# First loads in order of need on two queues, the fourth token tile transposed by DMA, and the last q tiles in passes of 128

## The chip, the cores and the metric

The kernel runs on one core of a Trainium2 chip. The time is device microseconds for one execution.

In the profile PE is TensorE's matmuls, PEld its weight loads, DVE is VectorE, ACT is ScalarE, SP is SyncE. "SPq" and "ACTq" are the sequencers of SyncE and ScalarE when they issue DMA. Times are microseconds from the start of the span.

## The reference

Two layers, each of a dilated sliding attention block and a gated feed-forward block, on 2048 tokens of width 1024. Both blocks add to the residual `x`, and both start with a layernorm.

```python
def _A_ref(x, wqkv, wo):            # attention: 32 heads of 32, window of 8 keys, step 2
    qkv = (x @ wqkv) ...            # q, k, v
    ...                             # softmax over the 8 keys, weighted sum of v
    return o @ wo
def _B_ref(x, w1, w3, w2):
    return (silu(x @ w1) * (x @ w3)) @ w2
x = x + _A_ref(_layernorm(x), wqkv, wo)
x = x + _B_ref(_layernorm(x), w1, w3, w2)
x = x + _A_ref(_layernorm(x), wqkv, wo)
x = x + _B_ref(_layernorm(x), w1, w3, w2)
```

## The kernel before

Tokens go in chunks of 512, that is four tiles of 128 (0 to 3). Everything is recorded as operations with an assumed length and with the keys they read and write. A list scheduler, `place()`, simulates the engines with these lengths and writes the instructions in the order that its simulation gives. The order on each engine is fixed by the simulation, not by what is ready on the chip. And an `after=` key that a load does not really read gives no wait on the chip: it only moves the load later in the issue order.

```python
def place(self, n_banks=8, rate=330e3):
    engines = ("PE", "DVE", "ACT", "SP", "AQ", "POOL")   # AQ: DMA issued by ScalarE
    ...                                                   # earliest start first; PE has lanes
    placed.sort(key=lambda o: (o.start, o.seq))

def dma(kb, dst, src, reads, writes, cls=3, transpose=False, queue="SP"):
    def emit(op):
        if queue == "AQ":
            nc.scalar.dma_start(dst, src)
        elif transpose:
            nc.sync.dma_start_transpose(dst, src)
        else:
            nc.sync.dma_start(dst, src)
    return pr.add(queue, 0.45, emit, reads, writes, cls, size=kb * 1024)
```

The start of the kernel is written by hand. The q weights come as eight "rows" of 256 KB (row k holds 128 input channels). Tiles 0 and 1 are projected with only the mean taken off (their scale is put in later), one row at a time, so that TensorE can start before all weights are there. Tiles 2 and 3 are normalised first. Then K and V of the chunk follow with full-width matmuls of 512 columns; K's weights are two loads of 1 MiB, which I call K's first and second half.

```python
def q_first():
    for hh in range(2):                                   # x0 in halves, on the two queues
        dma(128, x_sb[0][:, ...], xin[:, 0, ...], [], [("x", 0, hh)], 0, queue="AQ" if hh else "SP")
    dma(256, x_sb[1][:], xin[:, 1, :], [], [...], 0, queue="AQ")
    rows = q_weights(0, "k", load=False)
    for kk in range(4):
        rows[2](kk)                                       # rows 0 to 3, SyncE
    load_x(0, 2, 4)                                       # x2, x3, SyncE
    rows[2](4)
    rows[2](5)
    ...
    rows[2](6, 2, queue="AQ", after=[("part", 1)])        # rows 6 and 7, ScalarE
    ...
    for j in range(2, TPC):                               # tiles 2 and 3
        stats(j); root(j, j + 1); apply(j)
        transposed(xn[j], ...)                            # on TensorE, copied by DVE and ACT
    for j in range(2):                                    # tiles 0 and 1, for K and V
        ...
        dma(256, xnT[b][:, :, j * P:(j + 1) * P], xn[j][:], [("xn", j)], [("xnT", b, j)], 0, transpose=True)
    ...
    for g in range(4):                                    # q of tiles 2 and 3: 64 matmuls of 256 columns
        ...
    wslots[1] = q_weights(1, "s")                         # K's weights, two halves of 1 MiB
```

Of the kernel before, what the change touches and what calls it, by code (L numbers as in the profile page):

```python
# [156 lines left out]
def kernel(  # L157
# [11 lines left out]
    nc = tc.nc  # L169
    P = 128  # L170
    _, S, D = A_x.shape
    F = B_w1.shape[1]
    KT = D // P
# [41 lines left out]
    wo = alloc("wo", [P, KT, D])  # L215
# [38 lines left out]
# [9 lines that stand above are left out]
# [34 lines left out]
    def load_x(c, j0=0, j1=TPC, after=()):  # L297
        for j in range(j0, j1):
            n = c * TPC + j
            dma(256, x_sb[n][:], xin[:, n, :], after, [("x", n, 0), ("x", n, 1)], 0 if c == 0 else 3)  # L300
# [3 lines left out]
    def ln(c, first=False):  # L304
        s = stage_no[0]
        b, q = s % 2, s % 4
        xb = xnT[b]

        def stats(j, after=()):
            n = c * TPC + j  # L310
            pri = -9 if first else 1
            for hh in range(2):
                dve(0.67, lambda _, hh=hh: nc.vector.bn_stats(st[q][:, j, hh, :],  # L313
                                                              x_sb[n][:, hh * 512:(hh + 1) * 512]),
                    [("x", n, hh)] + list(after), [("st", q, j, hh)], pri)
            dve(0.2, lambda _: nc.vector.bn_aggr(mv[q][:, j, :], st[q][:, j, :, :]),  # L316
                [("st", q, j, 0), ("st", q, j, 1)], [("mv", q, j)], pri)

        def root(j0, j1):
            act(0.3, lambda _: nc.scalar.activation(sd[q][:, j0:j1], mv[q][:, j0:j1, 1], ACTF.Sqrt, bias=epst[:]),  # L320
                [("mv", q, j) for j in range(j0, j1)] + ["eps"], [("sd", q, j) for j in range(j0, j1)], -9 if first else 0, table="sqrt")
            dve(0.16, lambda _: nc.vector.reciprocal(rstd[q][:, j0:j1], sd[q][:, j0:j1]),
                [("sd", q, j) for j in range(j0, j1)], [("rstd", q, j) for j in range(j0, j1)], -9 if first else 0)

        def apply(j):
            n = c * TPC + j
            dve(0.5, lambda _: nc.vector.tensor_scalar(xn[j][:], x_sb[n][:], mv[q][:, j, 0:1], rstd[q][:, j:j + 1],  # L327
                                                       op0=ALU.subtract, op1=ALU.mult),
                [("x", n, 0), ("x", n, 1), ("mv", q, j), ("rstd", q, j)], [("xn", j)] + [("xn", j, h) for h in range(2)], -9 if first else 1)

        if first:
            return b, q, stats, root, apply
        for j in range(TPC):
            stats(j)
        root(0, TPC)
        for j in range(TPC):
            apply(j)
            dma(256, xb[:, :, j * P:(j + 1) * P], xn[j][:], [("xn", j)],
                [("xnT", b, j)] + [("xnT", b, j, h) for h in range(2)], 0, transpose=True)
        return b  # L340
# [14 lines left out]

    wslots = {}

    def q_weights(which, split, load=True, after=()):
        ids = [take_slot(), take_slot()]
        if not load:  # L360
            def row(kk, n=1, after=(), **kw):
                i = ids[kk // 4]
                v = slot[i][:].rearrange("p (k c) -> p k c", k=4)
                dma(256 * n, v[:, kk % 4:kk % 4 + n, :], wqkv_v[:, kk:kk + n, which * D:(which + 1) * D], after,
                    [("w", i, kk % 4 + z) for z in range(n)], 0, **kw)
            return ids, split, row
        for h, i in enumerate(ids):
            if split != "c":
                v = slot[i][:].rearrange("p (k c) -> p k c", k=4)
                dma(1024, v, wqkv_v[:, 4 * h:4 * h + 4, which * D:(which + 1) * D], after,  # L370
                    [("w", i, k) for k in range(4)], 3)
            else:
                v = slot[i][:].rearrange("p (k c) -> p k c", k=KT)
                dma(1024, v, wqkv_v[:, :, which * D + h * 512:which * D + (h + 1) * 512], [],
                    [("w", i, k) for k in range(4)], 3)
        return ids, split

    def q_lhs(ws, kk, m):
        ids, split = ws
        if split == "s":  # L380
            i = ids[kk // 4]
            return slot[i][:].rearrange("p (k c) -> p k c", k=4)[:, kk % 4, m::KT], ("w", i, kk % 4)
        if split == "k":
            i = ids[kk // 4]
            return slot[i][:].rearrange("p (k c) -> p k c", k=4)[:, kk % 4, m * P:(m + 1) * P], ("w", i, kk % 4)
        i = ids[m // 4]
        return (slot[i][:].rearrange("p (k c) -> p k c", k=KT)[:, kk, (m % 4) * P:(m % 4 + 1) * P],
                ("w", i, kk // 2))
# [47 lines left out]
    def q_first():  # L436
# [3 lines left out]
        dma(256, x_sb[1][:], xin[:, 1, :], [], [("x", 1, 0), ("x", 1, 1)], 0, queue="AQ")  # L440
        rows = q_weights(0, "k", load=False)
        wslots[0] = rows[:2]
        for kk in range(4):
            rows[2](kk)
        load_x(0, 2, 4)
        rows[2](4)
        rows[2](5)
        b, q, stats, root, apply = ln(0, first=True)
        ce = hT[:, 8:16, :]
        dve(0.45, lambda _: nc.vector.tensor_scalar(xn[2][:, 0:512], x_sb[0][:, 0:512], 0.0, 0.0, op0=ALU.add,  # L450
# [1 line left out]
            [("x", 0, 0)], [("xn", 2), ("part", 0)], -9)  # L452
        act(0.75, lambda _: nc.scalar.activation(xn[3][:, 0:512], x_sb[0][:, 512:1024], ACTF.Copy,
                                                 accum_out=part[:, 1:2]), [("x", 0, 1)], [("xn", 3), ("part", 1)], -9)
        rows[2](6, 2, queue="AQ", after=[("part", 1)])
        dve(0.16, lambda _: nc.vector.tensor_scalar(mean[:, 0:1], part[:, 0:1], part[:, 1:2], 1.0 / D, op0=ALU.add,
                                                    op1=ALU.mult), [("part", 0), ("part", 1)], [("mean", 0)], -9)
        act(1.15, lambda _: nc.scalar.activation(xn[3][:], x_sb[1][:], ACTF.Copy, scale=1.0 / D,
# [7 lines left out]
            transposed(xn[j], [("xn", j, h) for h in range(2)], ce[:, :, j * P:(j + 1) * P],  # L466
                       [("ce", j, k) for k in range(KT)])
        for j in range(2, TPC):
            stats(j)
            root(j, j + 1)  # L470
            apply(j)
            transposed(xn[j], [("xn", j)] * 2, xnT[b][:, :, j * P:(j + 1) * P],
                       [("xnT", b, j, k // 4) for k in range(KT)])
        for j in range(2):
            act(1.25, lambda _, j=j: nc.scalar.activation(sgt[j][:].rearrange("p a b -> p (a b)"), x_sb[j][:],
                                                          ACTF.Square, bias=mean[:, j:j + 1], scale=-1.0,
# [37 lines left out]
        store(pa, [op] * 4, 0)  # L514
        pa = [Acc() for _ in range(4)]
        ops = []
        for g in range(4):
            lk = [[q_lhs(wslots[0], kk, m)[0] for kk in range(KT)] for m in (2 * g, 2 * g + 1)]

            def emit(op, g=g, lk=lk, pa=pa):  # L520
                for m in range(2):
                    for kk in range(KT):
                        nc.tensor.matmul(bank[pa[g].bank][:, m * 2 * P:(m + 1) * 2 * P], lhsT=lk[m][kk],  # L523
                                         rhs=xnT[b][:, kk, 2 * P:4 * P], start=(kk == 0 and m == 0),
                                         stop=(kk == KT - 1), skip_group_check=True)
            ops.append(pr.add("PE", 16 * 0.1092, emit,
                              [("w", i, k) for i in wslots[0][0] for k in range(4)] +
                              [("xnT", b, j, h) for j in (2, 3) for h in range(2)],
                              [], takes=[pa[g]], lag=0.17))
        store(pa, ops, 2)  # L530
        for m0 in range(0, KT, 2):
            dma(256, spill_view(0, 0, m0, 0), hT[:, m0:m0 + 2, :],
                [("hT", m, j) for m in (m0, m0 + 1) for j in range(TPC)], [("d", 0, 0, 0, m0)], 1)
        wslots[1] = q_weights(1, "s")
        load_x(1, 0, 4, [("xn", 1)])
        load_x(2, 0, 2, [("xn", 1)])
        wslots[2] = q_weights(2, "s", after=[("xn", 1)])
        load_x(2, 2, 4, [("hT", 7, TPC - 1)])
        load_x(3, 0, 4, [("hT", 7, TPC - 1)])
        for which, key, tile_ in ((1, "kT", kT), (2, "vT", vT)):  # L540
            dve(0.11, lambda _, tile_=tile_: nc.vector.memset(tile_[:, :, 0:HALO], 0.0), [], [(key, "h")], 1)
            q_tile(0, 0, which, wslots[which], b, (key, tile_))
        for t0, t1_ in ((0, 2), (2, 4), (4, 5), (5, 6), (6, 7), (7, 8)):
            dma(256 * (t1_ - t0), wo[:, t0:t1_, :], wo_v[:, t0:t1_, :], [("d", 0, 2, 0, 6)], [("wo", t0)], 3)
        stage_no[0] += 1

# [24 lines left out]
    def t_stage(l, half):  # L571
# [54 lines left out]
        for j in range(TCH // P):  # L626
            n = tok0 // P + j
            for hh in range(2):
                a = Acc()
                op = mm8(a, [(oT[oh][:, t, j * P:(j + 1) * P], wo[:, t, hh * 512:(hh + 1) * 512]) for t in range(KT)],  # L630
                         True, True, [("oT", oh, t) for t in range(KT)] + [("wo", t) for t in (0, 2, 4, 5, 6, 7)], lane=1)
                xs = x_sb[n][:, hh * 512:(hh + 1) * 512]
                evac(dve, t1(512), lambda _, xs=xs, a=a: nc.vector.tensor_tensor(xs, xs, bank[a.bank][:], op=ALU.add),  # L633
                     op, [("x", n, hh)], [("x", n, hh)], a)
# [126 lines left out]
```

## Time and profile before

| | before |
|---|---|
| median, 6 runs | 1616.09 us (1615.79 to 1616.38) |
| span of the profiled run | 1614.2 us |
| PE busy | 1601.5 us (99%) |
| first full-width matmul (K of chunk 0) | 22.54 us |
| last matmul starts | 1611.16 us |

The page's first part gives each engine's busy time, its share and its instructions. Its fourth part is the chain of work that ended last. Of the kernel before:

```profile
PE 1601.5 (99%) x7463; PEld 762.6 (47%) x7610; DVE 1121.5 (69%) x1904; ACT 331.3 (21%) x527; POOL 5.2 (0%) x28
...
PE bank L347 98%; DMA slot<-in_A_wqkv_dram 1%; PE bank L523 0%; PE bank L509 0%; PE bank L428 0%; SPq L261 0%; DVE x L688 0%
```

L347 is the helper that makes all full-width matmuls. The one other item with a share is the DMA that brings the q weights. The timeline of the same kernel (start, duration, engine, line, operation, count, and in brackets the idle time of the engine before it with what ended it) shows where:

```profile
5.89 1.05 PE L509 MATMUL bank<-hT,slot 128*128 128x128 bf16 x16 [0.25 <-DVE hT L433]
6.96 0.62 PE L428 MATMUL bank<-ident,xn 128*128 128x128 bf16 x8
7.42 2.83 PE L509 MATMUL bank<-hT,slot 128*128 128x128 bf16 x40
11.16 2.79 PE L509 MATMUL bank<-hT,slot 128*128 128x256 bf16 x24 [0.91 <-DMA slot<-in_A_wqkv_dram]
13.79 1.06 PE L428 MATMUL bank<-ident,xn 128*128 128x128 bf16 x16
14.68 1.04 PE L509 MATMUL bank<-hT,slot 128*128 128x256 bf16 x8
15.56 7.15 PE L523 MATMUL bank<-xnT,slot 128*128 128x256 bf16 x64
22.54 22.82 PE L347 MATMUL bank<-xnT,slot 128*128 128x512 bf16 x102
```

L509 is the q of tiles 0 and 1, L428 are transposes, L523 is the q of tiles 2 and 3. There is one wait of size, 0.91 us for q weights. From 22.54 us on TensorE does not pause: the sum of its matmuls at their own pace is 1588.6 us, and the last one starts 1588.6 us later.

SyncE's issues in the same timeline:

```profile
5.71 1.97 SPq L261 DMA_DIRECT2D slot<-in_A_wqkv_dram  x4
13.87 3.85 SPq L259 DMA_TRANSPOSE xnT<-xn  x2
17.77 2.94 SPq L261 DMA_DIRECT2D x<-in_A_x_dram  x6
```

The four loads issued from 5.71 us are rows 4 and 5 and both halves of K's weights, the last that K needs from HBM. Then SyncE stands until tile 0 is normalised, and issues two DMA transposes.

### The profile page before, as it was taken

The page shows a single profiled execution, that of the slowest core. Times are in us where ns is not written, and L with a number is a line of the kernel's source. Part 1 is how long each engine was busy: PE and PEld are TensorE (multiplying, and loading weights), DVE is VectorE, ACT ScalarE, POOL GpSimd, SP SyncE. Part 2 cuts the span into 40 slices and gives each one's busy share as a digit, 9 for nine tenths or more (in the row PEclk, how much of TensorE's full clock was granted, in tenths as well). Part 3 has the DMA queues.
Part 4 walks back from the last instruction along what each step waited for, and adds up shares of the span by engine and source line. Part 5 has one row for each costly group of instructions (what it writes and reads, how often), then busy time and mean ns, then how long its engine had stood idle before and what let it go on. Part 6 is the DMA issues. An engine that isn't in the chain of part 4 may idle for free.

```text
span 1614.2 us, 19079 instructions
## 1 busy us (share of the span) xinstructions
PE 1601.5 (99%) x7463; PEld 762.6 (47%) x7610; DVE 1121.5 (69%) x1904; ACT 331.3 (21%) x527; POOL 5.2 (0%) x28
## 2 busy tenths in 40 slices
PE   9999999999999999999999999999999999999999
PEld 6555544444444444444444444444444444444444
DVE  5898888889889888888898729884288832211211
ACT  5423322021211222113211032110321101101110
POOL 1000000000000000000000000000000000000000
PEclk9999999999999999999999999999999999999999
DMA  9834755395548664758645487365873464454451
GB/s 320 228 100 150 224 170 171 118 225 168 171 136 251 195 190 132 217 167 234 189 136 160 160 243 231 122 173 176 253 221 119 158 181 156 144 176 150 156 165 44
DMA packets 350777, 285.80 MB, mean 177 GB/s; under 512 B 72288, under 2 KB 344928, under 8 KB 350688
## 3 DMA queue, kind: packets, MB, share of 16 engines
q1 hardware_dynamic: 350128, 283.67, 58.2%
q8 instruction: 59, 0.97, 0.2%
q10 hardware_dynamic: 560, 0.92, 0.2%
q14 instruction: 30, 0.25, 0.0%
HBM read 238.94 MB, written 29.36 MB: 166 GB/s over the span
## 4 chain that ended last, share of the span: by engine, by line
PE 99%; DMA 1%; issue 0%; SPq 0%; DVE 0%
PE bank L347 98%; DMA slot<-in_A_wqkv_dram 1%; PE bank L523 0%; PE bank L509 0%; PE bank L428 0%; SPq L261 0%; DVE x L688 0%
## 5 line engine op out<-in xcount | busy, mean ns | idle before, releaser
L347 PE MATMUL bank<-xnT,slot 128*128 128x512 bf16 x4955 | 1088.9, 379 | 5.3
L347 PEld LDWEIGHTS <-slot 128*128 128x128 bf16 x5056 | 518.1, 102 | 573.0
L347 PE MATMUL bank<-slot,hT 128*128 128x512 bf16 (+2 forms) x1812 | 387.3, 372 | 1.9
L658 DVE TENSOR_TENSOR hT<-sg,bank 128x512 bf16<-128x512 bf16 x224 | 153.4, 685 | 213.0 <-PE bank L347 196.3
L265 DVE TENSOR_TENSOR scr<-scr 128x1024 bf16<-128x1024 bf16 (+3 forms) x576 | 292.1, 535 | 2.1
L347 PEld LDWEIGHTS <-hT 128*128 128x128 bf16 x1848 | 178.5, 98 | 208.7
L656 ACT ACTIVATE sg<-bank 128x512 bf16<-128x512 f32 x224 | 133.8, 597 | 653.8 <-PE bank L347 613.6
L265 DVE TENSOR_TENSOR scr<-qT,kT 128x2048 bf16<-128x2048 bf16 x128 | 153.7, 1216 | 71.7 <-DMA kT<-qkv_d 70.1
L405 ACT CAST sgt<-bank 128x512 bf16<-128x512 f32 x184 | 107.9, 586 | 290.9 <-PE bank L347 273.1
L265 DVE TENSOR_TENSOR scr<-pA,vT 128x2048 bf16<-128x2048 bf16 x128 | 152.5, 1216 | 0.4
L688 DVE TENSOR_TENSOR x<-x,bank 128x512 bf16<-128x512 bf16 (+1 forms) x66 | 43.7, 669 | 122.7 <-PE bank L347 122.4
L347 PE MATMUL bank<-wo,oT 128*128 128x512 bf16 x502 | 112.6, 379 | 0.5
L313 DVE BATCH_NORM_STATS2 st<-x 128x6 f32<-128x512 bf16 x124 | 81.5, 679 | 11.5 <-DMA x<-in_A_x_dram 11.0
L347 PEld LDWEIGHTS <-oT 128*128 128x128 bf16 x512 | 50.1, 98 | 60.3
L633 DVE TENSOR_TENSOR x<-x,bank 128x512 bf16<-128x512 bf16 x64 | 43.9, 685 | 36.5 <-PE bank L347 35.0
L320 ACT ACTIVATE sd<-mv,epst 128x4 f32<-128x4 f32 (+1 forms) x17 | 5.1, 299 | 182.4 <-DVE mv L316 181.9
L616 DVE STREAM_TRANSPOSE pA<-pB 128x2048 bf16<-128x2048 bf16 x16 | 37.0, 2310 | 0.4
L593 DVE STREAM_TRANSPOSE pB<-pA 128x2048 bf16<-128x2048 bf16 x16 | 37.0, 2310 | 0.4
L656 ACT ACT_TABLE_LOAD x20 | 25.7, 1283 | 51.3 <-PE bank L347 51.1
L265 DVE TENSOR_TENSOR pA<-scr 128x256 bf16<-128x256 bf16 x128 | 35.3, 282 | 0.3
L327 DVE TENSOR_SCALAR xn<-x,mv,rstd 128x1024 bf16<-128x1024 bf16 x62 | 30.8, 541 | 4.6 <-DMA xnT<-xn 4.5
L265 DVE TENSOR_TENSOR oT<-scr 128x256 bf16<-128x256 bf16 x128 | 33.6, 282 | 0.1
(60 smaller groups left out, 210.0 us busy)
## 6 DMA issues: line engine op xcount, KB each, us to landing
slot<-in_B_w_dram SPq DMA_DIRECT2D x160, 1024.0 KB, 5.8
slot<-in_A_wqkv_dram SPq DMA_DIRECT2D x28, 1024.0 KB, 5.2
qkv_d<-sgt SPq DMA_DIRECT2D x92, 256.0 KB, 3.4
qT<-qkv_d SPq DMA_DIRECT2D x16, 512.0 KB, 5.0
slot<-in_B_w_dram SPq DMA_DIRECT2D x16, 512.0 KB, 5.5
kT<-qkv_d SPq DMA_DIRECT2D x14, 544.0 KB, 6.6
vT<-qkv_d SPq DMA_DIRECT2D x14, 544.0 KB, 5.7
out_dram<-x SPq DMA_DIRECT2D x31, 128.0 KB, 4.2
```

The lines of the kernel that those rows point to most:

```text
L265: return lambda _: nc.vector.tensor_tensor(o, a, b, op=op)
L313: dve(0.67, lambda _, hh=hh: nc.vector.bn_stats(st[q][:, j, hh, :], x_sb[n][:, hh * 512:(hh + 1) * 512]), [("x", n, hh)] + list(after), [( ...
L320: act(0.3, lambda _: nc.scalar.activation(sd[q][:, j0:j1], mv[q][:, j0:j1, 1], ACTF.Sqrt, bias=epst[:]), [("mv", q, j) for j in range(j0, ...
L327: dve(0.5, lambda _: nc.vector.tensor_scalar(xn[j][:], x_sb[n][:], mv[q][:, j, 0:1], rstd[q][:, j:j + 1], op0=ALU.subtract, op1=ALU.mult), ...
L347: nc.tensor.matmul(bank[a.bank][:, 0:ncol], lhsT=w, rhs=r, start=first and i == 0, stop=last and i == n - 1)
L405: evac(act, 0.59, lambda _, a=a, i=i, m=m: nc.scalar.copy(sgt[i][:, m % 2, :], bank[a.bank][:]), op, [], [("sgt", i, m % 2)], a)
L593: dve(2.31, lambda _: nc.vector.transpose(psmT[:].rearrange("p c d -> p (c d)"), psm[:].rearrange("p w s -> p (w s)")), allA, ["pB"])
L616: dve(2.31, lambda _: nc.vector.transpose(At[:].rearrange("p w s -> p (w s)"), AeT[:].rearrange("p c d -> p (c d)")), ["pB"], allA)
L633: evac(dve, t1(512), lambda _, xs=xs, a=a: nc.vector.tensor_tensor(xs, xs, bank[a.bank][:], op=ALU.add), op, [("x", n, hh)], [("x", n, hh) ...
L656: evac(act, 0.6, lambda _, i=i, a=ag: nc.scalar.activation(sg[i][:], bank[a.bank][:], ACTF.Silu), og, [], [("sg", i)], ag, table="silu")
L658: evac(dve, t1(512), lambda _, i=i, a=au, f=f: nc.vector.tensor_tensor(hT[:, f, :], sg[i][:], bank[a.bank][:], op=ALU.mult), ou, [("sg", i ...
L688: evac(dve, t1(cn), lambda _, xs=xs, a=a, cn=cn: nc.vector.tensor_tensor(xs, xs, bank[a.bank][:, 0:cn], op=ALU.add), op, [("x", n, hh)], [ ...
```

## The change

The intent: bring the q weights in the order in which TensorE needs them, so that the wait at 10 us goes; take eight transposes off TensorE by giving tile 3 to a DMA transpose; and make the q of tiles 2 and 3 in two passes of 128 columns, so that tile 2 can start while tile 3 is still on its way. The diff, cut to its core:

```diff
-        for kk in range(4):
+        for kk in (0, 1, 3, 4):
             rows[2](kk)
-        load_x(0, 2, 4)
-        rows[2](4)
+        rows[2](2, queue="AQ")
+        load_x(0, 3, 4)
         rows[2](5)
+        rows[2](6, 2)
...
-        rows[2](6, 2, queue="AQ", after=[("part", 1)])
+        dma(256, x_sb[2][:], xin[:, 2, :], [("part", 1)], [("x", 2, 0), ("x", 2, 1)], 0, queue="AQ")
...
-            transposed(xn[j], [("xn", j)] * 2, xnT[b][:, :, j * P:(j + 1) * P], ...)
+            if j == 2:
+                transposed(xn[j], [("xn", j)] * 2, xnT[b][:, :, j * P:(j + 1) * P], ...)
+            else:
+                dma(256, xnT[b][:, :, j * P:(j + 1) * P], xn[j][:], [("xn", j)], ..., 0, transpose=True)
...
-        for g in range(4):
-            ... 16 matmuls with rhs=xnT[b][:, kk, 2 * P:4 * P]
+        for j in (2, 3):
+            for g in range(4):
+                ... 16 matmuls with rhs=xnT[b][:, kk, j * P:(j + 1) * P]
...
-        wslots[1] = q_weights(1, "s")
+        wslots[1] = q_weights(1, "s", after=[[], [("xn", 3)]])
```

Two smaller edits are left out here: the statistics of tiles 2 and 3 are put after the first use of tile 1, and two of the loads of `wo` are joined.

## The prediction

> **What bounds it now.** TensorE: the page gives PE 99% busy; the chain of waits is 98% matmuls of the main helper and about 1% "DMA slot<-in_A_wqkv". In the timeline the first full-width matmul (K of chunk 0) starts at 22.54 us, and from there starts follow each other at 215.8 ns to 1611.2 us. That line has 7,416 matmuls (28 of the last of 256 columns, 56 of 128): 7,332 x 0.2158 + 28 x 0.109 + 56 x 0.056 = 1588.6 us, just what lies between. So nothing stalls PE after 22.54 us, and the whole question is when that matmul starts.
>
> **PE before 22.54 us.** From the first projection matmul at 5.89 us: 48 of 128 columns at 55.8 ns, 40 of 256 at 109.2 ns, 24 transposes at 55.8 ns, 64 of 256 for token tiles 2 and 3: 15.38 us. The other 1.27 us are waits: 0.19 for the transpose of tile 1, and 1.08 us from 10.09 to 11.16, for row 4 of the q weights. It landed at 11.11 because x2, x3 and rows 6 and 7 went ahead of it.
>
> **What the change does.**
> - Row 4 moves ahead of x3, x2, and rows 6-7. It should land near 8.5 us, row 5 near 10.4, rows 6-7 near 11.8 (the first loads are still 3 MiB, and all had landed at 11.79 before). Needed: about 10.3, 11.2, 12.1. The 1.08 us wait goes, with 0.3 us of margin for rows 6-7. That order and not the second queue gives this agrees with the Trainium skill, DMA: Bandwidth & Descriptors, "Issuing engines are not separate DMA queues".
> - Eight transposes leave PE: -0.45 us.
> - The q of tiles 2 and 3 takes 128 x 55.8 ns = 7.14 us instead of 64 x 109.2 = 6.99: +0.15. The Trainium skill (TensorE: Matmul & The Clock Gate, "Back-to-back issue gap") gives about 81 ns for a weight load and matmul pair at 128 columns[...]; this trace has 55.8 ns for such pairs, and I use the trace.
> - ScalarE's issue of x2 waits until row 0 has landed (4.96 us before) and stands ahead of its sum of x1, which began at 5.24: +0.2 us on tile 1's transposes.
>
> Sum: -1.08 - 0.45 + 0.15 + 0.2 = -1.2 us, all on the critical path. The first full-width matmul would start at about 21.35 us.
>
> **What can eat it.** SyncE now issues three DMA transposes (issue 1.35 to 2.15 us each, landing 4 to 5 us later in this stage) with the second half of K's weights between the first and second. Before, the last landed at 19.69 us; one more should move that to about 20.7 to 21, hardly before the need. I allow 0.2 us on average. Tile 3's transpose should land near 17 us and is needed at 17.8. Later, the output projections move by up to 40 matmuls, mostly later; their smallest slack before was 0.6 us, so I expect no new stall.
>
> **Prediction.** 1615.1 us, 8 in 10 between 1614.2 and 1616.1. Faster by over 2%: 0.005; within 2%: 0.99; slower: 0.005.
>
> **What would show it.** Right: no PE gap near 10 us; eight fewer transposes on PE; 128-column pairs at 56 ns; first full-width matmul at 21.1 to 21.8 us; no gap afterwards; the span shorter by as much. Wrong: a gap at the start of K (about 21 us) ended by the DMA transposes or K's second weights; a gap ended by rows 6-7 near 12 us or tile 3's transpose near 17.8 us; 128-column pairs at 65 ns or more (+1.2 us); a later gap at an output projection.

## The result, and the profile after

| | before | after |
|---|---|---|
| median, 6 runs each | 1616.09 us | 1620.47 us |
| runs | 1615.79 to 1616.38 | 1619.52, 1619.52, 1619.65 and 1621.28, 1621.29, 1621.31 |
| span of the profiled run | 1614.2 us | 1617.7 us |
| K of chunk 0 starts | 22.54 us | 25.22 us |
| last matmul starts | 1611.16 us | 1614.90 us |

The ratio is 1.0027 (interval 1.0014 to 1.0040). The change costs 4.4 us where I had expected a gain of 1. The runs after have two values, 1.7 us apart. The profiled one is of the lower value.

Of the changed kernel, the busy times and the chain of the page:

```profile
PE 1609.8 (100%) x7666; PEld 763.4 (47%) x7666; DVE 1119.5 (69%) x1903; ACT 328.2 (20%) x524; POOL 5.4 (0%) x28
...
PE bank L347 97%; DVE scr L265 1%; DMA xnT<-xn 0%; PE bank L514 0%; DMA x<-in_A_x_dram 0%; DVE xn L327 0%; PE bank L428 0%; SPq L259 0%; DVE pA L265 0%; ACT xn L454 0%; DVE x L640 0%; DVE st L313 0%; ACT xnT L433 0%; SPq L261 0%; ACT hT L503 0%
```

PE's busy time seems to have grown by 8 us, but that is a matter of records: the trace before lacks one matmul record in fifty, this one lacks none. The work is nearly the same. The timeline of the changed kernel (L514 is the q of tiles 0 and 1, L530 that of tiles 2 and 3):

```profile
6.77 1.21 PE L514 MATMUL bank<-hT,slot 128*128 128x128 bf16 x16 [0.22 <-DVE hT L433]
7.81 0.61 PE L428 MATMUL bank<-ident,xn 128*128 128x128 bf16 x8
8.26 5.45 PE L514 MATMUL bank<-hT,slot 128*128 128x128 bf16 x64
13.54 0.61 PE L428 MATMUL bank<-ident,xn 128*128 128x128 bf16 x8
13.99 1.04 PE L514 MATMUL bank<-hT,slot 128*128 128x256 bf16 x8
14.96 7.31 PE L530 MATMUL bank<-xnT,slot 128*128 128x128 bf16 x128
25.22 4.94 PE L347 MATMUL bank<-xnT,slot 128*128 128x512 bf16 x22 [2.96 <-DMA xnT<-xn]
```

The wait at 10 us is gone, and the q part ends 0.44 us earlier than before (22.10 against 22.54), although this run started its first projection 0.88 us later. Then TensorE stands for 2.96 us until a DMA transpose has landed. SyncE's issues show how it comes to be late:

```profile
7.33 1.36 SPq L261 DMA_DIRECT2D slot<-in_A_wqkv_dram  x3
14.13 1.35 SPq L259 DMA_TRANSPOSE xnT<-xn  x1
15.54 0.57 SPq L261 DMA_DIRECT2D slot<-in_A_wqkv_dram  x1
16.21 5.41 SPq L259 DMA_TRANSPOSE xnT<-xn  x2
```

The second half of K's weights, issued at 7.16 us before, is now issued at 15.54. It stands behind the transpose of tile 3 in SyncE's order, and is issued when the issue of that transpose has ended, at 15.49 us; the transpose had waited until DVE had normalised tile 3, at 14.06 us (the view of SyncE's waits puts 5.4 us down to this). The windows of both kernels from 14 to 18 us (busy times, then granted clock, DMA share and GB/s) show what this does to the DMA engines. Before:

```profile
14.00:18.00 4.00, 4.00 (x47) 3.67 (x45) 1.30 (x3) 3.53 (x7) 2.79 (x15) 1.00 1.16 242
```

And after, where in these 4 us less than half is moved:

```profile
14.00:18.00 4.00, 4.00 (x66) 3.82 (x64) 1.36 (x5) 2.54 (x5) 3.24 (x15) 1.00 0.62 113
```

The half load then lands at 21.77 us, 3.86 us later than before, and the two transposes behind it at 22.75 and 25.13. Not all of this follows from the order: the two transposes land 2.38 us apart, where it was 0.91 us before. From 23.2 to 24.4 us the DMA engines moved 35 GB/s; why, no run here shows. There is a second new wait, much later. In the timeline of the changed kernel:

```profile
172.02 7.07 PE L347 MATMUL bank<-wo,oT 128*128 128x512 bf16 x32
178.93 12.25 PE L347 MATMUL bank<-xnT,slot 128*128 128x512 bf16 x56
192.04 3.18 PE L347 MATMUL bank<-xnT,slot 128*128 128x512 bf16 x14 [0.87 <-DVE scr L265]
```

At 192 us the first feed-forward stage begins. The step there is 1.03 us longer than a matmul. The view names a DVE instruction, but that is not what was waited for: the last of this stage's four DMA transposes landed at 191.91 us, and PE's sequencer passed its DMA semaphores at 191.94. Before, the same transposes had landed at 187.47 us, about 0.85 us before their need, and the output projection (`bank<-wo,oT`) had ended earlier relative to this stage.

So for the profiled runs: +2.68 us at the start of K, +1.03 us at 192 us, and 0.18 us less in all the rest, most of it after the last matmul (2.85 us against 3.06): 3.53 us, the difference of the spans. The runs of the upper value have 1.7 to 1.8 us on top, which this trace does not show.

### The profile page after: what moved, and what is told of

Its sections match the earlier page's. It is cut to its first block, busy times and chain, and to the rows that moved or that the text cites. A ratio compares the mean times of both kernels' runs of the same rounds, so it can differ in the third digit from the quotient of the medians. Undisturbed runs are those within 1.5% of the kernel's fastest.

```text
span 1617.7 us, 19330 instructions
## 1 busy us (share of the span) xinstructions
PE 1609.8 (100%) x7666; PEld 763.4 (47%) x7666; DVE 1119.5 (69%) x1903; ACT 328.2 (20%) x524; POOL 5.4 (0%) x28
## 4 chain that ended last, share of the span: by engine, by line
PE 98%; DVE 1%; DMA 1%; ACT 0%; SPq 0%; issue 0%
PE bank L347 97%; DVE scr L265 1%; DMA xnT<-xn 0%; PE bank L514 0%; DMA x<-in_A_x_dram 0%; DVE xn L327 0%; PE bank L428 0%; SPq L259 0%; DVE pA L265 0%; ACT xn L454 0%; DVE x L640 0%; DVE st L313 0%; ACT xnT L433 0%; SPq L261 0%; ACT hT L503 0%
## 5 line engine op out<-in xcount | busy, mean ns | idle before, releaser
L663 ACT ACT_TABLE_LOAD x19 | 24.4, 1283 | 50.3 <-PE bank L347 50.1
```

The costliest lines, as they stand in the source:

```text
L663: evac(act, 0.6, lambda _, i=i, a=ag: nc.scalar.activation(sg[i][:], bank[a.bank][:], ACTF.Silu), og, [], [("sg", i)], ag, table="silu")
```

## The experiments

Fourteen experiments ran, with twelve kernels (e12 is the kernel of e8b again, e14 that of e11); all gave correct results. Times are medians of 4 or 5 runs, with those of the kernel before in the same rounds (1615.95 to 1616.02 us) beside them. Four submissions, e5 to e8, found no chip and ran again under new labels with the same text. This is what the traces show of the events in question (us; row 4 and rows 6 and 7 of the q weights, K's second half as issued and landed, the last transpose of chunk 0; read from the records of each DMA's landing):

```
                      row 1  row 4  6,7    K half 2        last T  K starts  time
before                 5.70  11.11   9.74   7.16 > 17.91   19.69   22.54    1616.09
after                  7.31   8.65  12.49  15.54 > 21.77   25.13   25.22    1619.5 or 1621.3
e1  half 2 first       7.39   8.72  13.95   8.77 > 19.27   22.32   23.76    1616.50
e2  tile 3 on PE       6.80   9.15  12.48   8.50 > 17.82   20.04   23.07    1616.00
e3  loads only         7.41   8.77  12.09   8.79 > 18.63   20.42   22.54    1615.54
e4  wait only          5.71  10.91   9.81   7.05 > 18.02   19.80   22.34    1615.73
e5b row 2 on SyncE     6.07   8.35  11.75  14.65 > 21.10   24.48   24.57    1620.50
e9  half 2 on ACT      5.93   8.05  11.42  10.85 > 18.57   21.66   23.18    1616.48
e10 e1, row 2 on SP    6.50   8.51  13.14   7.88 > 18.47   21.52   22.96    1615.98
e12 best               5.69   8.60  11.74   7.09 > 18.04   19.82   21.51    1615.14
```

In each of these traces SyncE issues its next load of weights (row 4 before and in e4, row 5 in the others) 0.01 to 0.02 us after row 1 has landed. So a late row 1 also delays the loads behind it.

### Which part makes K late: e1, e2, e3, e4

Theory A: the `after` key at K's second half holds it back. Theory B: the third DMA transpose on SyncE's queue is the cost by itself. A third candidate is the new order of loads.

e1, against the changed kernel:

```diff
-        wslots[1] = q_weights(1, "s", after=[[], [("xn", 3)]])
+        wslots[1] = q_weights(1, "s")
```

> The changed kernel, but the second half of K's weights does not wait for the normalised tile 3. Theory A (that wait puts 1 MiB of weights between the DMA transposes and is what holds the last transpose to 25.13 us): the second half lands near 18.5 us, the last transpose by about 21.5, K starts at 22.0 to 22.6 instead of 25.22, and the time falls from 1619.5 (its quick state) to 1616 to 1617. Theory B (the third DMA transpose on SyncE's queue is what holds it): last transpose still after 23.5 us, K after 23.5, time 1618 or more. If the wait of 2.96 us before K is what lets the granted clock fall in half of the runs (0.999, 1621.3 us), these runs have one value only and a clock of 1.0.

Measured: 1616.50 us (1615.70 to 1617.19), clock 1.0 in all runs. The half load is issued at 8.77 us and the last transpose lands at 22.32, before TensorE needs it. That is below theory B's 23.5, though above theory A's 21.5. K starts at 23.76, not at 22.0 to 22.6: other waits have taken the place, as the timeline of e1 shows.

```profile
7.44 0.62 PE L514 MATMUL bank<-hT,slot 128*128 128x128 bf16 x8 [0.73 <-DMA slot<-in_A_wqkv_dram]
14.00 1.05 PE L514 MATMUL bank<-hT,slot 128*128 128x256 bf16 x8 [1.08 <-DMA slot<-in_A_wqkv_dram]
20.19 3.73 PE L530 MATMUL bank<-xnT,slot 128*128 128x128 bf16 x64 [0.25 <-DMA xnT<-xn]
```

The first is for row 1, the second for rows 6 and 7, the third for tile 3's transpose: it was issued at 14.19 us, and landed at 20.15, just after the half load that now stands ahead of it. About 3 us of the loss are gone with one changed line, but the change gains nothing either.

e2, against the changed kernel:

```diff
-            if j == 2:
-                transposed(...)
-            else:
-                dma(256, xnT[b][...], xn[j][:], ..., transpose=True)
+            transposed(...)                      # tiles 2 and 3 on TensorE, as before
```

> The changed kernel, but tile 3 is transposed on TensorE as before, so SyncE has two DMA transposes; K's second half still waits for the normalised tile 3. Theory A: the second half is still issued near 14 us and lands near 19 to 20, the last transpose at 22 to 23, K at 22.5 to 23.5, time 1617 to 1618.5. Theory B: last transpose by 21.5, K at 22.3 to 22.6 (eight transposes more on TensorE), time 1616 to 1616.5.

Measured: 1616.00 us (1615.31 to 1616.50), K at 23.07, last transpose at 20.04 us. The time and the last transpose fit theory B; K does not (22.3 to 22.6 was expected; this trace waits 0.37 us for DVE's normalisation of tile 2). But neither theory had been put to the test: the half load was issued at 8.50 us although its `after` key was still there. Its wait is no wait on the chip. The key only puts it behind tile 3's normalisation in the order, and without a DMA transpose of tile 3 nothing on SyncE stands ahead of it. Both parts together make the loss: the key puts the load behind the transpose, the transpose waits for DVE.

e4 fell for the same reason. Its edit is the `after` key alone, in the kernel before:

```diff
-        wslots[1] = q_weights(1, "s")
+        wslots[1] = q_weights(1, "s", after=[[], [("xn", 3)]])
```

> The kernel before, with only the wait of K's second half of weights for the normalised tile 3. Theory A: issued near 13.9 us instead of 7.16, it lands at 19.5 or later instead of 17.91, the last transpose at 21.5 to 23.5 instead of 19.69; K waits up to 1 us: time 1616.3 to 1617.3. Theory B: the last transpose stays at or before 21.5 us, no wait before K, time 1616.1.

Measured: 1615.73 us (1615.61 to 1615.91). The load was issued at 7.05 us, so nothing was delayed, and what I had written for theory A does not follow from it.

e3 is the kernel before with only the new loads (the first two hunks of the diff above).

> The kernel before with only the new order and queues of the first loads. Theories A and B both: no wait near 10 us on TensorE; K at 22.54 - 1.08 plus what the later first tile costs (x0 landed at 3.97 instead of 3.28 us, first projection matmul 0.88 us later in the changed kernel): 22.2 to 22.5, time 1615.7 to 1616.1. Theory C (the late x0 is chance and not the loads): x0 at 3.3 us, K at 21.5, time 1615.0.

Measured: 1615.54 us (1615.21 to 1615.80), K at 22.54 us, the same as before to 0.01 us. x0 landed at 3.27 and 3.55 us, so its late landing in the trace of the changed kernel was chance. But the gain of 1.08 us did not come. The timeline of e3:

```profile
5.90 0.61 PE L510 MATMUL bank<-hT,slot 128*128 128x128 bf16 x8 [0.25 <-DVE hT L433]
7.46 0.62 PE L510 MATMUL bank<-hT,slot 128*128 128x128 bf16 x8 [0.95 <-DMA slot<-in_A_wqkv_dram]
8.36 5.45 PE L510 MATMUL bank<-hT,slot 128*128 128x128 bf16 x64
```

The wait has moved from row 4 at 10 us to row 1 at 7.4 us, and is as long. (The profiled run is the slowest of e3's four; their median is 0.41 us below the kernel before, which this trace does not explain.)

### Why row 1 is late, and what the order is worth: e5b, e8b, e12

In every trace with row 2 on ScalarE's queue row 1 lands at 6.80 to 7.41 us instead of 5.70. Theory D: the two queues are served side by side, so row 2, issued at the same time on the other queue, takes its share from row 1. e5b keeps row 2 on SyncE in the changed kernel:

```diff
-        for kk in (0, 1, 3, 4):
+        for kk in (0, 1, 2, 3, 4):
             rows[2](kk)
-        rows[2](2, queue="AQ")
```

> The changed kernel, but row 2 of the q weights stays on SyncE's queue, so ScalarE's holds x0's half, x1 and x2. Theory D (a third load on ScalarE's queue takes half of the rate from row 1, and row 1's landing also frees SyncE's next issue, row 5): row 1 lands near 5.7 us as before instead of 6.8 to 7.4, row 5 is issued near 5.8 instead of 7.3, all first loads by 11.9. Theory A', the order on SyncE (K's second half stands behind the transpose of tile 3, which waits for DVE): K still starts late, 23.5 to 25, time 1618 to 1619.5 or, with the lower clock, 1621. If the loads were the cause, K at 22 and 1616.

Measured: row 1 at 6.07 us, row 5 issued at 6.08, rows 6 and 7 at 11.75; K at 24.57, 1620.50 us (1620.28 to 1620.68) with the lower clock in all four runs. Theory D holds: in all traces with row 2 on SyncE row 1 lands at 5.68 to 6.50 us. And the loads are not what makes K late.

The same loads in the kernel before, with tiles 2 and 3 as they were, are e8b, and again e12 with more rounds. Against the kernel before:

```diff
-        for kk in range(4):
+        for kk in (0, 1, 2, 3, 4):
             rows[2](kk)
-        load_x(0, 2, 4)
-        rows[2](4)
+        load_x(0, 3, 4)
         rows[2](5)
+        rows[2](6, 2)
...
-        rows[2](6, 2, queue="AQ", after=[("part", 1)])
+        dma(256, x_sb[2][:], xin[:, 2, :], [("part", 1)], [("x", 2, 0), ("x", 2, 1)], 0, queue="AQ")
```

> The kernel before with only the new order of loads, all of the weights on SyncE's queue and x2 on ScalarE's; tiles 2 and 3 as before. Theory D: no wait near 7.4 us nor near 10 us, K starts at 21.3 to 21.8, time 1614.8 to 1615.3, below before and below e3.

> The kernel of e8 again, with more rounds: the version that may beat both. K at 21.3 to 21.8, median 1615.1, before 1616.0, that is 0.05% less.

Measured: 1615.17 us (one run of four at 1616.45, the others 1614.97 to 1615.34), then 1615.14 us (1614.98 to 1615.51) beside 1615.98 (1615.57 to 1616.21). The ratio of the second is 0.9995, with an interval of 0.9983 to 1.0008 that holds 1; but in e12's rounds no run of one kernel reaches into the range of the other. The timeline of e12 has no wait for weights at all:

```profile
5.76 1.05 PE L509 MATMUL bank<-hT,slot 128*128 128x128 bf16 x16 [0.25 <-DVE hT L433]
7.34 5.50 PE L509 MATMUL bank<-hT,slot 128*128 128x128 bf16 x64
14.53 7.15 PE L523 MATMUL bank<-xnT,slot 128*128 128x256 bf16 x64
21.51 4.70 PE L347 MATMUL bank<-xnT,slot 128*128 128x512 bf16 x20
```

K starts 1.03 us earlier than before, nearly the whole wait of 1.08 us. (This is the fastest of e12's five runs; the medians differ by 0.84 us.) So the order of need was right and worth nearly what it was predicted to be worth; its split over two queues undid it.

### Can the transpose of tile 3 pay at all: e9, e10

e9 takes e5b and issues K's second half from ScalarE at 10.85 us, so that neither stands behind the other in an order:

```diff
-        wslots[1] = q_weights(1, "s", after=[[], [("xn", 3)]])
+        wslots[1] = q_weights(1, "s", after=[[], [("part", 1)]])     # and queue="AQ" for this half
```

All DMA transposes stay on SyncE. The Trainium skill (DMA: Bandwidth & Descriptors, "Silent corruption: two transposing streams in flight at once") warns of transposes from both queues in flight together; no run here tries it.

> The changed kernel with row 2 on SyncE's queue, and with the second half of K's weights issued from ScalarE, near 11 to 12 us, so that on no queue it stands behind the transpose of tile 3, nor that behind it. Theory A' (the late K comes from the in-order SyncE, where the second half waits behind the transpose of tile 3, which waits for DVE): the half lands by 19, the transposes near 16.5, 19 and 21, K starts at 21.2 to 21.8, time 1614.7 to 1615.4, clock 1.0. If three DMA transposes by themselves were the cost, the last would still land after 23 and K start after it: 1617.5 or more.

Measured: 1616.48 us (1616.06 to 1616.61), K at 23.18. The last transpose landed at 21.66 us, so three transposes alone are not the 3 us. But the other half of the expectation failed: tile 3's transpose, issued at 12.88 us, landed at 19.56 instead of near 16.5, and TensorE waited for it. The timeline of e9:

```profile
14.28 3.74 PE L529 MATMUL bank<-xnT,slot 128*128 128x128 bf16 x64
19.61 3.73 PE L529 MATMUL bank<-xnT,slot 128*128 128x128 bf16 x64 [1.59 <-DMA xnT<-xn]
```

e10 is e1 with row 2 on SyncE.

> The changed kernel with row 2 on SyncE's queue and K's second half ahead of the transpose of tile 3 on SyncE. As in e1 tile 3's transpose now follows 2 MiB of weights and lands at 19 to 20, after the need at about 17.8: a wait of 1 to 2 us in the passes of tile 3, K at 22 to 23, time 1615.8 to 1616.8. So with one queue one of the two is late either way.

Measured: 1615.98 us (1615.70 to 1616.60), K at 22.96. Both are as expected, but not for the reason expected: tile 3's transpose landed at 19.35 and cost a wait of 0.43 us, not 1 to 2; rows 6 and 7, at 13.14 us, cost 1.17 us at 13.2. Without that second wait K would have started near 21.8 us (an estimate, 22.96 - 1.17), which is still not before e12's 21.51.

A pattern runs through all these traces: a DMA transpose that is issued while a load of 1 MiB is under way does not land until that load has landed, whether it stands on the same queue or (e9) on the other. The first transpose behind K's second half came 0.87 to 1.09 us after it in all sixteen traces (0.87 us before, 0.98 in the changed kernel, 0.99 in e9, 1.09 in e2). Tile 3's transpose in the changed kernel, which had only the rest of K's first half beside it (landed at 15.89), took 3.22 us from issue to landing; no transpose in any trace took less than 3.07. The transposes do not simply queue behind the load, though: in the kernel before, 391 of the 405 packets that started from 16 to 17 us were small ones of under 512 B, which appear with the transposes, while the load of K's second half, with nothing else big left, landed only at 17.91. Why the DMA engines behave so no run here shows.

It explains the dilemma: tile 3 is needed near 18 us, K's second half is needed near 21 us and takes until 18 at best. If the load goes first, tile 3 is late; if tile 3 goes first, the load stands behind DVE, and the transposes of tiles 0 and 1 behind the load. None of the three orders tried (the change, e1 with e10, and e9) kept the 0.45 us of TensorE that the transpose saves. K's second half in smaller loads, or behind all three transposes, was not tried.

### The passes of 128: e11

The kernel before with only the loop over `j in (2, 3)` of the diff.

> The kernel before with only the passes of 128 columns for tiles 2 and 3. If 128-column pairs run at 55.8 ns there too: K at 22.54 + 0.15 = 22.7, time 1616.1 to 1616.3; if they are held by weight loads (65 ns or more), K at 23.7 or later, 1617.2.

Measured: 1617.09 us (1616.59 to 1617.39). From the end of the wait for row 4 to the start of K it is 11.54 us (11.46 to 23.01), where before it is 11.38 (11.16 to 22.54): the passes cost 0.16 us, as predicted (0.15); e14, the same kernel, gives 11.54 again. That is not the whole difference. This trace also waits at the first feed-forward stage, by 0.82 us, which I come to below.

### The two values: e7b

In the traces of e5b and e6b the granted clock is seen to fall. The start of K in e5b and in e6b, with the wait before it:

```profile
24.57 1.78 PE L347 MATMUL bank<-xnT,slot 128*128 128x512 bf16 x4 [3.12 <-DMA xnT<-xn]
25.31 0.41 PE L347 MATMUL bank<-xnT,slot 128*128 128x512 bf16 x1 [2.61 <-DMA xnT<-xn]
```

Windows of e5b (us, PE, PEld, DVE, ACT, POOL busy, then the granted clock, DMA share, GB/s):

```profile
24.00:25.00 1.00, 0.41 (x1) 0.35 (x3) 0.00 (x0) 0.00 (x0) 0.00 (x0) 1.00 1.07 350
25.00:28.00 3.00, 2.97 (x8) 1.30 (x8) 2.64 (x6) 0.33 (x1) 0.00 (x0) 0.53 1.00 289
28.00:29.00 1.00, 1.00 (x5) 0.45 (x4) 1.00 (x3) 0.53 (x2) 0.00 (x0) 0.70 1.01 371
29.00:33.00 4.00, 4.00 (x21) 2.63 (x20) 2.93 (x10) 1.92 (x5) 0.00 (x0) 1.00 1.05 391
```

The clock records of e5b give 0.5 for 3.41 us, from 25.18 us on, just after the wait; those of e6b the same 3.41 us from 25.64. Half of 3.41 is 1.7 us, the distance of the two values. The Trainium skill (TensorE: Matmul & The Clock Gate, "What's actually happening") describes a gate with two states that looks at TensorE's activity in free-running windows of 3413 ns; both traces have a stretch of 3413 ns at 0.5. That the windows run freely no run here shows. The same page puts the rule as no idle gaps over about 3.4 us ("HAM oscillation — how this bites in real kernels"); here 2.61 us (e6b) were enough, while 2.96 us in the profiled run of the changed kernel left the clock alone.

e7b puts ten unused matmuls on constants into the wait of the changed kernel:

```diff
+        for _ in range(10):
+            pr.add("PE", 0.0, lambda op: nc.tensor.matmul(bank[op.takes[0].bank][:], lhsT=one[:, 0:P], rhs=one,
+                                                          start=True, stop=True), takes=[Acc()])
```

> The changed kernel with ten matmuls on constants ahead of K, in the wait of 2.96 us, results unused. Theory F (the idle TensorE lets the granted clock fall in some runs, depending on phase; that is the second value of 1621.3 us): all runs near 1619.5 to 1620, clock 1.0 in all. Rival: two values as before.

Measured: K at 25.05, as late as ever, 1619.29 us (1618.49 to 1619.77), and a clock of 1.0 in all four runs. Two lines of e7b's timeline (L539 makes the unused matmuls), and its window that can be held against e5b's:

```profile
22.00 2.35 PE L539 MATMUL bank<-const-bfloat16-1.0 128*128 128x512 bf16 x9
25.05 1.24 PE L347 MATMUL bank<-xnT,slot 128*128 128x512 bf16 x5 [0.70 <-DMA xnT<-xn]
25.00:28.00 3.00, 2.96 (x14) 2.02 (x14) 2.46 (x5) 0.86 (x2) 0.00 (x0) 1.00 1.06 313
```

In the same rounds the two kernels with the open wait (e5b, e6b) had 0.999 in all eight. In all other experiments, whose longest wait of TensorE before K was 1.59 us (e9), every run had 1.0. The second value comes from the idle time, and the upper 1.7 us of the loss are a consequence of the late K.

### The wait at 192 us: e6b, e13, e14

Theory E: in the scheduler's simulation K starts earlier than on the chip, so it puts the first two output projections behind 400 full-width matmuls instead of 384. The layernorm of the first feed-forward stage needs their result, and TensorE's count up to that stage is the same, so it gets 16 matmuls, 3.5 us, less time. e6b lets the scheduler believe in longer passes, nothing else:

```diff
-                ops.append(pr.add("PE", 16 * 0.0558, emit,
+                ops.append(pr.add("PE", 16 * 0.0558 + (0.85 if j == 3 else 0.0), emit,
```

> The changed kernel; only the length that its scheduler assumes for four of the q passes is raised, by 0.85 us each, so that the first output projections stand where they stood before (after 384 full-width matmuls instead of 400). Theory E (the projections moved 16 matmuls later leave the layernorm of the first feed-forward stage 3.5 us less, and this is the wait of 1.03 us at 192 us): that wait is gone, K still starts at 24 to 25.3, time 1618.5 instead of 1619.5 (and 1620.3 with the lower clock). Rival: the wait stays, time unchanged.

Measured: the wait fell from 1.03 to 0.55 us, it did not go; 1620.90 us with the lower clock in all runs. The edit did not do what was expected of it: in the trace the projections stand behind 392 matmuls, not 384. But e1, e2, e4 and e10 have them behind 392 too and do not wait there. So the place of the projections is not the whole of it. e13 makes the opposite trial, in the kernel of e12, which has no late K: the assumed length of the four q passes is lowered by 0.7 us each, which puts the projections behind 400 matmuls.

> The kernel of e8 and e12; only the length that its scheduler assumes for the four q passes of tiles 2 and 3 is lowered, by 0.7 us each, so that the first two output projections stand 16 full-width matmuls later, as in the changed kernel (after 400). Theory E (this place alone makes the wait of about 1 us before the first feed-forward stage): K starts at 21.5 as in e12, a wait of 0.8 to 1.2 us near 188 us ended by the DMA transposes, time 1616.0 to 1616.4. Rival (it needs the late K or the throttled clock): no such wait, 1615.1.

Measured: K at 21.52 us, 1616.09 us (1615.82 to 1616.33), and the timeline of e13 has the wait:

```profile
169.79 5.56 PE L347 MATMUL bank<-wo,oT 128*128 128x512 bf16 x25
175.19 12.25 PE L347 MATMUL bank<-xnT,slot 128*128 128x512 bf16 x56
188.32 6.85 PE L347 MATMUL bank<-xnT,slot 128*128 128x512 bf16 x31 [0.88 <-DVE scr L265]
```

The step is 1.04 us longer than a matmul, and the time is 0.95 us above e12's. The edit moves more than the projections (the two weight loads ahead of the stage are issued 6.9 us earlier than in e12), but these loads had landed by 176.18 us, and the first of the stage's transposes was issued at 180.24, 3.3 us later than in e12. So the later place is enough to make it.

It is not needed for it. e11 has the projections where they were before, and waits 0.82 us. e14 is e11's kernel once more:

> The kernel of e11 once more. There a wait of 0.8 us at the first feed-forward stage stood although the projections are where they were before (after 384). If that is chance (the second load of 1 MiB ahead of the transposes took 8.85 us to land there, 7.41 in the kernel before), this trace or some of its runs are without it: K at 22.7, times from 1616.2 up; if it belongs to the program, the wait is there again and all runs are 1616.9 or more.

Measured: 1616.88 us (1616.55 to 1617.17), and a wait of 0.64 us in the trace, with K at 22.46. So it belongs to that program, both traces of which have it (two of the four runs lie below the 1616.9 us expected for this case). In e11, e14 and e6b the second of two loads of 1 MiB ahead of these transposes took 8.6 to 8.9 us to land, in the kernel before and in e3 and e12 7.4 to 7.5, although the order of issues around it is the same; the transposes then land behind it. Why that load is slower in these programs stays open.

## Why the prediction was wrong

It said 1615.1 us with 1614.2 to 1616.1; measured were 1619.5 and 1621.3. Point by point:

- **"Nothing stalls PE after 22.54 us, and the whole question is when that matmul starts"**: right for the kernel before, and it gave the right place to look.
- **The wait for row 4 (-1.08)**: it went, and row 4 landed at 8.65 us, where 8.5 was predicted. But I took the second queue to be neutral. Row 1 came at 7.31 us instead of 5.70. In e3's trace K starts where it did before, to 0.01 us; with row 2 on SyncE (e12) 1.03 us are kept. I named the Trainium skill (DMA: Bandwidth & Descriptors, "Issuing engines are not separate DMA queues") for a second queue bringing no gain by itself, and the runs agree: the first loads had all landed at 12.09 us in e3 and at 11.74 in e12, which has one queue for the weights. But two loads issued side by side both came late (rows 1 and 2 at 7.41 and 7.94 us in e3, at 5.69 and 7.08 in e12), and this I did not draw from it.
- **Eight transposes (-0.45), passes (+0.15)**: the passes cost 0.16 us (e11). The page's 81 ns for a pair did not apply; the pairs ran at 55.8 ns, as the trace before had shown. The eight transposes did leave TensorE.
- **ScalarE's issue of x2 (+0.2)**: in e3 its sum of x1 begins at 5.50 us, 0.26 later than before, as sized, but TensorE stood for row 1 until 7.46 anyway.
- **The step that failed** is "one more should move that to about 20.7 to 21, hardly before the need. I allow 0.2 us on average." The last transpose landed at 25.13 us, and the wait was 2.96 us. I had counted the transpose as more of the same work on a busy DMA queue. In fact SyncE stood until 14.13 us for DVE, and the second half of K's weights stood behind it: the load was issued 8.4 us later than before, the DMA engines moved 113 GB/s from 14 to 18 us instead of 242, and K's half, landing 3.86 us later, held the two transposes behind it. (Another 1.5 us came between these two, and stays unexplained.) I had seen the order on SyncE, K's half "between the first and second" transpose, and did not ask what that order would wait for. e1 and e5b show it from both sides.
- **"Tile 3's transpose should land near 17 us"**: 17.35 us, right by luck: only because the big load was held back for it. Wherever the load went first, it landed at 19.35 to 20.15.
- **"I expect no new stall" later**: wrong by 1.03 us. I looked at the slack of the output projections themselves (0.6 us) and not at that of the layernorm that follows them. Its last transpose had about 0.85 us; counted from the start of K, the first is issued 3.5 us later than before and the last lands 1.8 us later. e13 shows that the later place is enough.
- **The clock** I did not think of. It adds 1.7 us in the runs in which it falls (three of six), and e7b, where the wait is filled and none of four runs has it, shows that it comes from the wait.

## What to carry to other kernels

Before a DMA that waits for compute is put on an in-order queue, ask what stands behind it: a load with no dependency of its own can end up waiting for an engine that it has nothing to do with, and the DMA engines then move little while they are needed (here 113 GB/s from 14 to 18 us instead of 242). Two loads issued at the same time on two queues both landed late here (rows 1 and 2 in e3), so what is needed first should stand first on one queue, and the other queue should get what is needed later. And a change that shortens the start in a scheduler's simulation moves work far behind it, so check the slack of every chain that the moved work feeds, not only its own.

## What the Trainium skill lacked or had wrong

- TensorE: Matmul & The Clock Gate, "Back-to-back issue gap", gives about 81 ns for a stream of weight loads and matmuls at 128 columns. Here 128 such pairs (after, L530) started every 55.8 ns.
- The same page, "HAM oscillation — how this bites in real kernels", puts the limit at idle gaps over about 3.4 us. Here the clock fell to half after waits of 2.61 us (e6b) and 3.12 us (e5b), and did not after 2.96 us (after), so shorter gaps are a risk too. The stretches of 3.41 us at half clock agree with the window and the two states that the page gives.
- DMA: Bandwidth & Descriptors, "Issuing engines are not separate DMA queues", says that the queues interleave and that a second issuing engine only saves issue time. It does not spell out that this also changes when a load lands: row 1 at 6.80 to 7.41 us with row 2 on the other queue, 5.68 to 6.50 us without.
- No page that I read tells how a DMA transpose fares beside plain loads: here the first transpose behind K's second half landed 0.87 to 1.09 us after that load of 1 MiB, on either queue, up to 6.8 us after its own issue (e5b), where no transpose in any trace took less than 3.07 us.
